# A decode attention kernel: the MLP spread over the first attention steps, K and V loaded in pairs

## The chip, the cores and the metric

One core of a Trainium2 chip. Times are device microseconds (us), medians of several executions. One profiled execution stands behind each trace; its span is about 2 us shorter than the time of the same execution (1378.4 us and 1380.39 us before).

## The reference

Two branches for 8 tokens, one per sequence, mixed by a gate. Branch A is attention over a cache: 32 heads, 4096 keys of 128, all bf16. The K cache and the V cache are 268 MB each. Branch B is a layernorm and an MLP (576 to 4608 to 576).

```python
q = (x @ wq).reshape(B, 1, 32, 128)                 # B = 8, x is [8, 1, 576]
scores = einsum("bhqd,bhkd->bhqk", q, k_cache) * 128 ** -0.5
a = einsum("bhqk,bhkd->bhqd", softmax(scores), v_cache) ... @ wo
b = gelu(layernorm(x) @ w1 + b1) @ w2 + b2          # w1 [576, 4608], w2 [4608, 576]
out = g * a + (1 - g) * b                           # g = sigmoid(sum(x * gate_w))
```

## The kernel before

An item is one (sequence, head): 1 MB of K and 1 MB of V, 256 items in all. K arrives with keys on the partitions, so TensorE transposes it (32 transposes an item) into PSUM, VectorE and ScalarE evacuate it (copy it to SBUF, the on-chip memory), and eight score matmuls follow. PV for an item (its softmax weights times V) runs LAG = 37 steps later, when the softmax of its sequence is done. `P.add` appends an operation to an engine's program together with the events it waits for; each engine runs its program strictly in order.

```python
NK = 5            # K slots of one item
NV = 6            # V slots of one item
...
# prologue, in program order; K loads go on the sync engine's queue, the rest on ScalarE's
dma wq -> w2reg ; dma w1 -> w1reg                    # ScalarE's queue
for n in range(min(NK, NITEM)):
    issue_k(n, waits=[])                             # sync engine's queue
...
# query projection (QT), 160 matmuls, waits for wq
P.add("act", lambda a: a.dma_start(w2_v, B_w2...), waits=[e_QT])     # w2 overwrites wq
# first MLP matmul (hT), 180 matmuls, waits for w1; GELU; second MLP matmul, waits for w2
...
for m in range(min(NV, NITEM)):                      # V slots lie where w1 and w2 were
    issue_v(m, waits=[ev_w2reg_free, ev_w1reg_free, e_mlp_sb])
...
def emit_T(n):                                       # transpose item n, then refill its slot
    ...
    if n + NK < NITEM:
        issue_k(n + NK, waits=[last_group_ev])
...
emit_T(0)
for s in range(last_step + 1):
    for (fn, b) in chain_at.get(s, []): fn(b)        # softmax of a sequence
    if s + 1 < NITEM: emit_T(s + 1)
    if s < NITEM: emit_S(s)                          # scores
    if 0 <= s - LAG < NITEM: emit_PV(s - LAG)        # frees a V slot: issue_v(m + NV)
# wo is loaded into the K slots after the last scores; final projection; output
```

(Cuts are marked; `dma wq -> ...` abbreviates the load calls.)

## Time and profile before

| what | value |
|---|---|
| time | 1380.15 us (1379.28 to 1381.33, 5 runs) |
| bytes moved by DMA | 559.55 MB |
| TensorE busy | 80% of the span |
| chain of waits that ended last | DMA 73%, TensorE 23% |

The page's view of 40 equal slices (34.5 us each) gives busy tenths for TensorE and the DMA engines, and the rate that the DMA engines moved:

```profile
PE   0789998888888888888888888888888888887335
...
DMA  9789999999999999999999999999999999999993
GB/s 332 268 335 425 418 389 425 425 424 425 425 426 425 425 426 424 426 425 425 425 425 425 424 426 424 424 422 419 420 423 422 420 418 425 418 421 357 420 420 167
```

The DMA row is full while TensorE has room, and the rate is flat at about 425 GB/s except at both ends. The chain of waits says the same: DMA has 73% of it, TensorE 23%. The view by stretches shows where the rate is lower. Each row gives the start and end of a stretch, its length, the busy time and count of each engine, and, in the last three columns, TensorE's granted clock, the DMA share and GB/s:

```profile
core 0: us, PE busy (x) PEld busy (x) DVE busy (x) ACT busy (x) POOL busy (x), PEclk, DMA share, GB/s
20.00:45.00 25.00, 10.31 (x160) 9.18 (x160) 1.27 (x1) 0.00 (x0) 0.00 (x0) 1.00 1.01 377
45.00:60.00 15.00, 11.43 (x180) 10.23 (x180) 0.00 (x0) 0.00 (x0) 0.00 (x0) 1.00 1.01 352
60.00:76.00 16.00, 12.63 (x107) 6.44 (x105) 4.88 (x11) 1.93 (x3) 0.00 (x0) 1.00 0.06 10
76.00:165.00 89.00, 80.10 (x1232) 60.50 (x1232) 54.07 (x83) 42.50 (x42) 0.00 (x0) 0.98 1.01 422
165.00:195.00 30.00, 27.89 (x492) 21.51 (x491) 18.38 (x31) 14.42 (x16) 0.00 (x0) 1.00 0.97 378
195.00:1200.00 1005.00, 855.83 (x14690) 690.29 (x14687) 380.23 (x581) 284.38 (x291) 0.00 (x0) 0.82 1.01 424
1200.00:1262.00 62.00, 52.22 (x944) 42.19 (x941) 22.79 (x34) 16.19 (x16) 0.00 (x0) 0.83 0.96 388
1262.00:1378.40 116.40, 49.74 (x1230) 39.94 (x1230) 4.25 (x11) 1.36 (x3) 0.00 (x0) 0.55 0.84 345
```

A way to read it: the kernel must move its bytes, and at 425 GB/s that takes 559.55 MB / 425 GB/s = 1316.6 us. The rest of the 1378.4 us, 61.8 us, is time in which the engines moved less than that. For one stretch the loss is length x (1 - rate / 425): 15.6 us at 60 to 76 us, 5.4 us at 1200 to 1262, about 22 us from 1262 to the end. This is a bookkeeping against the rate that the middle sustains, not a law: rates are rounded to 1 GB/s, which is 2.4 us over the long middle.

The 15.6 us are visible in order of time (columns: start, length, engine, line, operation, and in brackets the idle time before it with what ended it):

```profile
32.29 10.31 PE L366 MATMUL psum_all<-xT,w2reg 128*128 128x8 bf16 x160 [19.78 <-DMA w2reg<-in_A_wq_dram]
...
48.57 11.59 PE L383 MATMUL psum_all<-yT,w1reg 128*128 128x8 bf16 x180 [5.97 <-DMA w1reg<-in_B_w_dram]
...
62.02 0.44 ACT L399 ACTIVATE hb<-hb 128x288 f32<-128x288 f32 x1 [49.23 <-DVE hb L398]
...
63.10 0.59 PE L406 MATMUL psum_all<-w2reg,hT 128*8 128x512 bf16 x1 [2.94 <-DVE hT L401]
...
74.44 2.76 ACTq L305 DMA_DIRECT2D w2reg<-in_A_v_cache_dram  x5
```

The first MLP matmul starts when w1 lands (48.6 us), GELU comes at 62 us, the second matmul at 63.1 us, and only at 74.4 us does ScalarE issue the first V loads. All earlier loads were done by about 61 us: the five K slots were full and TensorE, still in the MLP, freed none. The queues were empty.

### The profile page before, as it was taken

To read this page: it belongs to the slowest core of one execution; us is meant where nothing else is said; L and a number is where in the kernel's file an instruction comes from. 1 tells how busy PE (TensorE), PEld (TensorE's weight loads), DVE (VectorE), ACT (ScalarE), POOL (GpSimd) and SP (SyncE) were. 2 spreads that over 40 slices of the span, in tenths; PEclk is the share of its full clock that TensorE was granted. 3 is DMA by queue.
4 is the path that set the end of the run, shared out by engine and by line. 5 is a ranking of instruction groups with operands and counts; after the bars stand their busy time and mean duration, and the time that the engine had idled before them with its cause. 6 is when DMAs were issued, how large, how long until landed. Compare 5 with 4: busy or idle time off the path is not lost.

```text
span 1378.4 us, 40050 instructions
## 1 busy us (share of the span) xinstructions
PE 1100.9 (80%) x19030; PEld 880.9 (64%) x19030; DVE 493.3 (36%) x762; ACT 364.1 (26%) x379; POOL 3.3 (0%) x12
## 2 busy tenths in 40 slices
PE   0789998888888888888888888888888888887335
PEld 0557777667667766767666666667666666766333
DVE  2146654343333433334333433334333343332000
ACT  0035543223222322223222232223222232222000
POOL 0000000000000000000000000000000000000000
PEclk9999998777887787778887788878888788877556
DMA  9789999999999999999999999999999999999993
GB/s 332 268 335 425 418 389 425 425 424 425 425 426 425 425 426 424 426 425 425 425 425 425 424 426 424 424 422 419 420 423 422 420 418 425 418 421 357 420 420 167
DMA packets 84002, 559.55 MB, mean 406 GB/s; under 512 B 8416, under 2 KB 17152, under 8 KB 17152
## 3 DMA queue, kind: packets, MB, share of 16 engines
q10 hardware_dynamic: 42752, 283.82, 49.8%
q1 hardware_dynamic: 40992, 273.18, 47.6%
q8 instruction: 149, 2.44, 0.6%
q0 software_dynamic: 96, 0.01, 0.0%
q14 instruction: 13, 0.11, 0.0%
HBM read 556.96 MB, written 0.01 MB: 404 GB/s over the span
## 4 chain that ended last, share of the span: by engine, by line
DMA 73%; PE 23%; ACT 2%; DVE 1%; issue 0%; ACTq 0%; DVEq 0%
DMA kregion<-in_A_k_cache_dram 63%; PE psum_all L487 16%; DMA w2reg<-in_A_v_cache_dram 7%; DMA w1reg<-in_B_w_dram 3%; PE psum_all L510 3%; PE psum_all L588 2%; ACT kregion L471 2%; PE psum_all L383 1%; PE psum_all L629 1%; PE psum_all L406 1%; ACT w1reg L545 0%; ACTq L305 0%; DVE kregion L472 0%; ACT w1reg L471 0%; PE psum_all L559 0%
## 5 line engine op out<-in xcount | busy, mean ns | idle before, releaser
L487 PE MATMUL psum_all<-identB,kregion 128*128 128x128 bf16 x8192 | 651.5, 249 | 169.9 <-DMA kregion<-in_A_k_cache_dram 147.0
L487 PEld LDWEIGHTS psum_all<-identB,kregion 128*128 128x128 bf16 x8192 | 583.3, 114 | 219.2 <-DMA kregion<-in_A_k_cache_dram 164.3
L472 DVE COPY kregion<-psum_all 128x1024 bf16<-128x1024 bf16 x687 | 459.5, 689 | 669.6 <-PE psum_all L487 662.3
L471 ACT COPY kregion<-psum_all 128x1024 bf16<-128x1024 bf16 x337 | 341.0, 1012 | 816.9 <-PE psum_all L487 803.2
L588 PEld LDWEIGHTS psum_all<-w1reg,w2reg 128*128 128x128 bf16 x6848 | 188.9, 98 | 152.9 <-issue 98.0
L588 PE MATMUL psum_all<-w1reg,w2reg 128*128 128x1 bf16 x6848 | 207.2, 164 | 52.0 <-DMA w2reg<-in_A_v_cache_dram 51.6
L510 PE MATMUL psum_all<-kregion,qmask 128*32 128x512 bf16 x2048 | 185.5, 439 | 0.0
L510 PEld LDWEIGHTS psum_all<-kregion,qmask 128*32 128x32 bf16 x2048 | 34.8, 98 | 34.0 <-issue 15.8
L588 PEld LDWEIGHTS psum_all<-w1reg 128*128 128x128 bf16 x1344 | 37.1, 98 | 29.4 <-issue 18.7
L588 PE MATMUL psum_all<-w1reg 128*128 128x1 bf16 x1344 | 40.7, 164 | 10.2 <-DMA w1reg<-in_A_v_cache_dram 10.2
L572 DVE RECIPROCAL rinv<-psum_all 128x32 f32<-128x32 f32 x8 | 2.9, 358 | 99.7 <-PE psum_all L569 99.7
L366 PE MATMUL psum_all<-xT,w2reg 128*128 128x8 bf16 (+1 forms) x160 | 10.3, 176 | 19.8 <-DMA w2reg<-in_A_wq_dram 19.8
L366 PEld LDWEIGHTS psum_all<-xT,w2reg 128*128 128x128 bf16 (+1 forms) x160 | 9.2, 107 | 20.9 <-DMA w2reg<-in_A_wq_dram 19.9
L383 PE MATMUL psum_all<-yT,w1reg 128*128 128x8 bf16 (+1 forms) x180 | 11.6, 176 | 6.0 <-DMA w1reg<-in_B_w_dram 6.0
L383 PEld LDWEIGHTS psum_all<-yT,w1reg 128*128 128x128 bf16 (+1 forms) x180 | 10.3, 107 | 7.3 <-DMA w1reg<-in_B_w_dram 6.1
L399 ACT ACTIVATE hb<-hb 128x288 f32<-128x288 f32 x1 | 0.4, 443 | 49.2 <-DVE hb L398 49.2
L406 PE MATMUL psum_all<-w2reg,hT 128*8 128x512 bf16 x36 | 10.4, 420 | 2.9 <-DVE hT L401 2.9
L374 DVE CAST qmask<-psum_all 128x256 bf16<-128x256 f32 x1 | 1.3, 1273 | 31.0 <-PE psum_all L366 31.0
L629 PE MATMUL psum_all<-kregion,oT_all 128*8 128x512 bf16 x32 | 10.9, 471 | 0.9 <-DVE oT_all L575 0.9
L471 ACT COPY w1reg<-psum_all 128x1024 bf16<-128x1024 bf16 x7 | 7.1, 1012 | 15.2 <-PE psum_all L559 15.2
L550 DVE TENSOR_SCALAR Rmat<-Emat,lpart 128x32 f32<-128x32 f32 x8 | 1.9, 241 | 25.0 <-ACT w1reg L545 25.0
L522 DVE TENSOR_REDUCE pmax<-psum_all 128x1 f32<-128x1024 f32 x8 | 9.7, 1218 | 2.6 <-PE psum_all L510 2.6
(72 smaller groups left out, 95.2 us busy)
## 6 DMA issues: line engine op xcount, KB each, us to landing
kregion<-in_A_k_cache_dram SPq DMA_DIRECT2D x256, 1024.0 KB, 21.9
w2reg<-in_A_v_cache_dram ACTq DMA_DIRECT2D x214, 1024.0 KB, 23.0
w1reg<-in_A_v_cache_dram ACTq DMA_DIRECT2D x42, 1024.0 KB, 23.4
w2reg<-in_B_w_dram ACTq DMA_DIRECT2D x1, 5184.0 KB, 19.0
w1reg<-in_B_w_dram ACTq DMA_DIRECT2D x1, 4608.0 KB, 42.1
kregion<-in_A_wo_dram SPq DMA_DIRECT2D x1, 4608.0 KB, 87.9
w2reg<-in_A_wq_dram ACTq DMA_DIRECT2D x1, 4096.0 KB, 28.2
w1reg<-in_B_w_dram ACTq DMA_DIRECT2D x1, 576.0 KB, 44.5
```

The lines of the kernel that those rows point to most:

```text
L366: e_QT = P.pe_write(lambda t, h=h, kc=kc, csz=csz: t.matmul(QT_ps[:, h * 8:h * 8 + B], lhsT=wq_v[0:csz, kc, h * Dh:(h + 1) * Dh], rhs=xT[0 ...
L383: e_hT = P.pe_write(lambda t, fc=fc, kc=kc, csz=csz: t.matmul(hT_ps[:, fc * 8:fc * 8 + B], lhsT=w1_v[0:csz, kc, fc * 128:(fc + 1) * 128], ...
L406: P.pe_write(lambda t, fc=fc: t.matmul(mlp_ps0[0:B, :], lhsT=hTv[:, fc, :], rhs=w2_v[:, fc, 0:512], start=(fc == 0), stop=(fc == NFC - 1)) ...
L471: return P.eng_read("act", lambda a, dst=dst, src=src: a.copy(dst, src), regions=[f"ring{r}"], waits=waits, pub=True)
L472: return P.eng_read("dve", lambda v, dst=dst, src=src: v.tensor_copy(dst, src), regions=[f"ring{r}"], waits=waits, pub=True)
L487: lambda t, r=r, jl=jl, j=j, kb=kb: t.transpose(ring[r][:, jl * 128:(jl + 1) * 128], kb[:, j, :], identB[:, :]),
L510: lambda t, q=q, i=i, jstart=jstart, b=b, h=h, sset=sset, kt=kt: t.matmul(S_ps[sset][32 * q:32 * q + 32, 512 * i:512 * i + 512], lhsT=qmas ...
L522: max_ev[b] = P.eng_read("dve", lambda v, b=b, sset=sset: v.tensor_reduce(pmax[:, b:b + 1], S_ps[sset][:, 0:1024], AX.X, ALU.max), regions ...
L550: R_ev[b] = P.add("dve", lambda v: v.tensor_scalar(Rmat[:, 32 * b:32 * b + 32], Emat[:, :], lpart[:, b:b + 1], None, ALU.mult), waits=[exp ...
L572: e1 = P.eng_read("dve", lambda v: v.reciprocal(rinv[:, 32 * b:32 * b + 32], acc[:, ACC_LBC:ACC_LBC + 32]), regions=["acc"], waits=[c4_ev[ ...
L588: lambda t, j=j, q=q, jj=jj, vb=vb, pt=pt, sl=sl, h=h: t.matmul(acc[:, 32 * sl + h:32 * sl + h + 1], lhsT=vb[:, j, :], rhs=pt[:, jj * 128 ...
L629: P.pe_write(lambda t, h=h: t.matmul(attn_ps0[0:B, :], lhsT=oT_v[:, h, 0:B], rhs=wo_v[:, h, 0:512], start=(h == 0), stop=(h == H - 1)), re ...
```

## The change

Intent: let TensorE begin with K at once and do the MLP in pieces between the first K items, so that the load queues always have work; and load K and V in pairs of heads, 2 MB each, into deeper buffers. wq moves into w1's region, w1 is loaded after the query projection, w2 gets its own region, and K pairs 2 and 3 wait for wq so that wq is not slowed.

```diff
-NK = 5
-NV = 6
+NKP = 4
+NVP = 4
+STEP_HT, STEP_GELU, STEP_MLP = 8, 16, 18
...
-    for n in range(min(NK, NITEM)):
-        issue_k(n, waits=[])
+    for kp in range(min(NKP, NPAIR)):
+        issue_k(kp, waits=([] if kp < 2 else [ev_wq]))
...
-        src = A_k_cache[bb, hh].rearrange("(p j) d -> p (j d)", p=128)
+        src = A_k_cache[bb, hh:hh + 2].rearrange("t (p j) d -> p t (j d)", p=128)
...
-        if n + NK < NITEM:
-            issue_k(n + NK, waits=[last_group_ev])
+        if n % 2 == 1 and (n // 2) + NKP < NPAIR:
+            issue_k((n // 2) + NKP, waits=[last_group_ev])
...                                     (V the same)
+    for n in range(min(NKT, NITEM)):
+        emit_T(n)                       # two items transposed before the query projection
+    prologue_QT()                       # then w1 and w2 are issued
...
+        for c in range(nchunk):         # 36 blocks of 128 hidden columns, 6 at a time
+            fcs = list(range(c * CH, min(NFC, (c + 1) * CH)))
+            pro_at.setdefault(STEP_HT + c, []).append(lambda fcs=fcs: prologue_hT(fcs))
+            pro_at.setdefault(STEP_MLP + c, []).append(lambda fcs=fcs: prologue_mlp(fcs))
+        pro_at.setdefault(STEP_GELU, []).append(prologue_gelu)
...
     for s in range(last_step + 1):
+        for fn in pro_at.get(s, []):
+            fn()
```

V pairs 0 and 1 (in w1's region) are issued after the last piece of the first matmul, pairs 2 and 3 (in w2's region) after the second.

## The prediction

> **What bounds the kernel now.** DMA bytes: the page counts 559.55 MB. By stretches (windows view): 0-60 us, 343 GB/s at a DMA share of 0.98; 60-76 us, 10 GB/s at 0.06; 76-182 us, 417 GB/s; 182-1240 us, 423 GB/s at 1.01; 1240-1262 us, 325 GB/s at 0.86; 1262-1357 us, 415 GB/s; 1357-1378 us, 32 GB/s. The chain of waits agrees: 73% DMA, 63% of it K loads. TensorE, 80% busy, works in the shadow of the loads: K and V of an item are 2.1 MB, 4.9 us at 425 GB/s, against 1085/256 = 4.2 us of matmul (transpose, score and PV groups). The Trainium skill (DMA: Bandwidth & Descriptors, Specifications) gives a fabric ceiling of 435 GB/s; the measured 423-425 is near it, so the middle has 2-3% to give at most.
>
> **What the change does.** (a) It moves the MLP (11.6 us first matmul, 3 us GELU, about 11 us second matmul) from the serial prologue into steps 8-23 of the K stage, and puts two K transposes before the query projection. (b) It joins K and V loads into pairs of 2 MB; a pair of slots is freed after its second item. Bytes and 8 KB rows stay. (c) Buffers grow from 5 K and 6 V items to 8 and 8. (d) w1 and w2 load after the query projection, K pairs 2 and 3 after wq.
>
> **What it is worth.** The gap at 60-76 us is the prize: there the five K slots are full, V waits for the MLP, and TensorE has not started on K. Afterwards K slots turn over from about 40 us while w1, w2 and K keep the queues filled: 15-16 us back. The rest of the MLP's 25 us was already covered by loads. Deeper buffers may recover 2-3 us of small losses (165-195 us, at 349-398 GB/s; 420 late).
>
> Against it: a bubble of about 2 us where wq lands and K pairs 2-3 are only then issued; 2-4 us in the K stage, where TensorE is already 4.8 of 5 us busy (2.6 us an item) and now also carries the MLP; 1 us at the end, where the last load brings two items. The end stays: 21 us after the last load, and the dip when K runs out.
>
> The pairs themselves I value at nothing: the engines show a share of 1.01 already, and where large wq pieces load beside K (16-28 us) the rate is about 427 GB/s, no better.
>
> Sum: 1380 - 15.5 - 2.5 + 4 = **1366 us**, range 1356 to 1374 (8 in 10). Chance of over 2% faster 0.12, within 2% 0.86, over 2% slower 0.02.
>
> **What would show it.** Right: no stretch near zero GB/s between 15 and 100 us; first PV at about 165-170 us instead of 184; the middle still at 423-425 GB/s; 20-22 us after the last load; mean DMA rate about 410 GB/s. If pairs mattered, the middle would run above 428. If the K stage became TensorE-bound, 100-180 us would fall below 400 GB/s.
>
> **What would make it wrong.** A middle 1% faster or slower with 2 MB loads is worth 11-13 us by itself. TensorE stalling in program order on w1 or w2 (steps 8 and 18) until the K slots are full would bring part of the gap back. The granted clock was 1.00 until about 215 us, then 0.82; if it drops earlier because TensorE works from 18 us on, the K stage loses several us.

## The result

The changed kernel takes 1365.82 us (1364.69 to 1366.2, 7 runs) against 1381.33 us for the kernel before in the same rounds (13 runs). The ratio is 0.9887, with a 95% interval of 0.9877 to 0.9898: 1.1% faster. A ratio here is the mean time of one kernel's runs over that of the other's of the same rounds, so it is not quite the ratio of the quoted medians.

The slices after (34.1 us each), and then the view by the same stretches (columns as before):

```profile
PE   3789998888878878888787988887888797887335
...
DMA  8999999999999999999999999999999999998993
GB/s 288 397 400 418 420 425 425 426 425 425 425 425 426 425 426 426 425 425 426 425 425 425 426 426 425 425 425 426 424 425 425 420 413 425 425 404 344 421 421 162
```

```profile
20.00:45.00 25.00, 13.33 (x188) 11.37 (x189) 2.08 (x3) 2.18 (x3) 0.00 (x0) 0.55 0.88 342
45.00:60.00 15.00, 14.58 (x223) 11.02 (x221) 9.79 (x15) 7.38 (x8) 0.00 (x0) 0.96 1.02 429
60.00:76.00 16.00, 6.55 (x95) 5.54 (x90) 2.67 (x4) 1.73 (x2) 0.00 (x0) 0.71 1.02 333
76.00:165.00 89.00, 83.95 (x1227) 62.51 (x1226) 47.97 (x77) 34.33 (x36) 0.00 (x0) 0.98 1.02 416
165.00:195.00 30.00, 28.19 (x539) 22.30 (x536) 16.55 (x27) 14.02 (x16) 0.00 (x0) 1.00 1.01 425
195.00:1200.00 1005.00, 831.84 (x14704) 679.58 (x14701) 379.69 (x583) 284.19 (x291) 0.00 (x0) 0.83 1.01 425
1200.00:1262.00 62.00, 49.98 (x959) 40.49 (x958) 20.39 (x33) 14.79 (x17) 0.00 (x0) 0.75 0.92 369
1262.00:1363.30 101.30, 38.91 (x1049) 31.96 (x1046) 2.27 (x5) 0.00 (x0) 0.00 (x0) 0.55 0.81 334
```

The second and third slices went from 268 and 335 to 397 and 400 GB/s; the chain of waits is still DMA's, 73%. The mean rate over the span rose from 406 to 410 GB/s. The losses by stretch, worked out as above from the two tables of stretches (the first 20 us lose 6.2 us in both):

| stretch, us | lost before, us | lost after, us | change |
|---|---|---|---|
| 20 to 45 | 2.8 | 4.9 | +2.1 |
| 45 to 60 | 2.6 | -0.1 | -2.7 |
| 60 to 76 | 15.6 | 3.5 | -12.2 |
| 76 to 165 | 0.6 | 1.9 | +1.3 |
| 165 to 195 | 3.3 | 0.0 | -3.3 |
| 195 to 1200 | 2.4 | 0.0 | -2.4, as large as the rounding |
| 1200 to 1262 | 5.4 | 8.2 | +2.8 |
| 1262 to the end | 21.9 | 21.7 | -0.2 |

The changes sum to -14.6 us; the spans differ by 15.1 us. The bytes are the same (559.52 MB), and the page's count of packets under 512 bytes fell from 8416 to 4320: 4096 fewer, 16 for each of the 256 loads that no longer exist.

Three rows of the timeline after explain the start: the query projection, the first piece of the MLP, and the first V loads:

```profile
30.30 10.31 PE L384 MATMUL psum_all<-xT,w1reg 128*128 128x8 bf16 x160 [10.66 <-DMA w1reg<-in_A_wq_dram]
...
72.19 1.98 PE L414 MATMUL psum_all<-yT,w1reg 128*128 128x8 bf16 x30 [9.45 <-DMA w1reg<-in_B_w_dram]
...
97.57 4.59 ACTq L319 DMA_DIRECT2D w1reg<-in_A_v_cache_dram  x2
```

The query projection starts at 30.3 us, when wq is in. TensorE then stands 9.4 us for w1 at 62 to 72 us, but in that stretch the DMA share is 1.02, so the stall costs nothing by itself. Issuing the first two V loads took ScalarE 4.59 us instead of 0.37 us each as in the middle. The first PV starts at 179.0 us, against 186.5 before.

### The profile page after: what moved, and what is told of

It is laid out like the page before. It is cut to its first block, busy times and chain, and to the rows that moved or that the text cites. A ratio compares the mean times of both kernels' runs of the same rounds, so it can differ in the third digit from the quotient of the medians.

```text
span 1363.3 us, 39656 instructions
## 1 busy us (share of the span) xinstructions
PE 1074.6 (79%) x19030; PEld 871.7 (64%) x19030; DVE 492.3 (36%) x762; ACT 364.3 (27%) x380; POOL 3.3 (0%) x12
## 2 busy tenths in 40 slices
DMA packets 79904, 559.52 MB, mean 410 GB/s; under 512 B 4320, under 2 KB 13056, under 8 KB 13056
## 4 chain that ended last, share of the span: by engine, by line
DMA 73%; PE 23%; ACT 2%; DVE 1%; ACTq 1%; issue 0%; DVEq 0%
DMA kregion<-in_A_k_cache_dram 62%; PE psum_all L530 14%; DMA w2reg<-in_A_v_cache_dram 7%; PE psum_all L631 3%; PE psum_all L553 3%; DMA w1reg<-in_B_w_dram 2%; DMA w1reg<-in_A_wq_dram 2%; ACT ktregion L510 1%; PE psum_all L414 1%; PE psum_all L384 1%; PE psum_all L693 1%; PE psum_all L444 1%; ACTq L319 0%; DVE ktregion L511 0%; PE psum_all L602 0%
## 5 line engine op out<-in xcount | busy, mean ns | idle before, releaser
L511 DVE COPY ktregion<-psum_all 128x1024 bf16<-128x1024 bf16 x687 | 458.8, 689 | 694.2 <-PE psum_all L530 687.2
L510 ACT COPY ktregion<-psum_all 128x1024 bf16<-128x1024 bf16 x337 | 341.0, 1012 | 828.9 <-PE psum_all L530 828.6
L553 PE MATMUL psum_all<-ktregion,qmask 128*32 128x512 bf16 x2048 | 178.2, 423 | 1.4 <-DVE qmask L392 1.4
L631 PEld LDWEIGHTS psum_all<-w1reg,w2reg 128*128 128x128 bf16 x4096 | 112.4, 98 | 89.1 <-issue 55.0
L631 PEld LDWEIGHTS psum_all<-w1reg 128*128 128x128 bf16 x4096 | 112.0, 98 | 86.0 <-issue 55.5
L631 PE MATMUL psum_all<-w1reg,w2reg 128*128 128x1 bf16 x4096 | 122.7, 164 | 33.7 <-DMA w2reg<-in_A_v_cache_dram 32.3
L631 PE MATMUL psum_all<-w1reg 128*128 128x1 bf16 x4096 | 122.2, 164 | 29.9 <-DMA w1reg<-in_A_v_cache_dram 29.9
L553 PEld LDWEIGHTS psum_all<-ktregion,qmask 128*32 128x32 bf16 x2048 | 34.4, 97 | 33.9 <-issue 12.6
L384 PE MATMUL psum_all<-xT,w1reg 128*128 128x8 bf16 (+1 forms) x160 | 10.3, 175 | 10.7 <-DMA w1reg<-in_A_wq_dram 10.7
L384 PEld LDWEIGHTS psum_all<-xT,w1reg 128*128 128x128 bf16 (+1 forms) x160 | 9.2, 107 | 11.9 <-DMA w1reg<-in_A_wq_dram 10.8
L510 ACT COPY w1reg<-psum_all 128x1024 bf16<-128x1024 bf16 x7 | 7.1, 1012 | 16.8 <-PE psum_all L602 16.8
## 6 DMA issues: line engine op xcount, KB each, us to landing
kregion<-in_A_wo_dram SPq DMA_DIRECT2D x1, 4608.0 KB, 92.2
```

What stands on the lines that cost most here:

```text
L384: e_QT = P.pe_write(lambda t, h=h, kc=kc, csz=csz: t.matmul(QT_ps[:, h * 8:h * 8 + B], lhsT=wq_v[0:csz, kc, h * Dh:(h + 1) * Dh], rhs=xT[0 ...
L510: return P.eng_read("act", lambda a, dst=dst, src=src: a.copy(dst, src), regions=[f"ring{r}"], waits=waits, pub=True)
L511: return P.eng_read("dve", lambda v, dst=dst, src=src: v.tensor_copy(dst, src), regions=[f"ring{r}"], waits=waits, pub=True)
L553: lambda t, q=q, i=i, jstart=jstart, b=b, h=h, sset=sset, kt=kt: t.matmul(S_ps[sset][32 * q:32 * q + 32, 512 * i:512 * i + 512], lhsT=qmas ...
L631: lambda t, j=j, q=q, jj=jj, vb=vb, pt=pt, sl=sl, h=h: t.matmul(acc[:, 32 * sl + h:32 * sl + h + 1], lhsT=vb[:, j, :], rhs=pt[:, jj * 128 ...
```

## The experiments

Twelve kernels ran. All gave the reference's result within the tolerance; one of them, rem128, computes part of it wrongly, which the comparison did not see. "Theory A" below is the prediction's: only empty load queues cost time. "Theory C" is its rival: the size of the loads or the depth of the buffers speeds up the middle.

### Parts of the change, one at a time

**split**: every 2 MB load becomes two of 1 MB, same moment, same slots, same release.

```diff
-        src = A_k_cache[bb, hh:hh + 2].rearrange("t (p j) d -> p t (j d)", p=128)
-        ... one dma_start of the pair
+        for t in range(2):
+            ... one dma_start of item 2 * kp + t, with its own semaphore      (V the same)
```

> The changed kernel with every 2 MB load issued as two loads of 1 MB, at the same moment, into the same slots, released in pairs as before. Theory A: nothing, 1364 to 1367 us, the middle at 422 to 425 GB/s. Theory C (the size of a load matters): 1372 us or more and a lower rate in the middle.

Measured: 1366.83 us, ratio to before 0.9897 (0.9884 to 0.9911); the middle (195 to 1200 us) at 425 GB/s, as after. The size of a load is worth nothing here. Theory C loses half of its ground.

**single**: no pairs at all; eight K and eight V slots of one item, each refilled as soon as it is free.

```diff
-        if n % 2 == 1 and (n // 2) + NKP < NPAIR:
-            issue_k((n // 2) + NKP, waits=[last_group_ev])
+        if n + 8 < NITEM:
+            issue_k(n + 8, waits=[last_group_ev])                             (V the same)
```

> The changed kernel with 1 MB loads, each issued as soon as its own slot is free (eight K and eight V slots, no pairs at all). Theory A: the loads of the middle stay the same, the dip where K runs out (1220 to 1250 us, 7.8 us lost with pairs, 5.4 us before) shrinks by 2 to 3 us: 1361 to 1364 us. Theory C: 1372 us or more.

Measured: 1365.13 us, ratio 0.9887 (0.9874 to 0.9901). It is no slower, so Theory C is out for pairs; but the expected 2 to 3 us at the end of K did not come: 1200 to 1262 us ran at 375 GB/s (7.3 us lost, against 8.2 with pairs and 5.4 before; the 7.8 us quoted above are for 1220 to 1250 us alone). The dip is not made by the pairs.

**shallow**: as single, but with the old depth of five K and six V slots. This is the spread MLP with the early transposes, and nothing else of the change.

```diff
+NKS = 5           # K slots of one item
+NVS = 6           # V slots of one item (slots 0 to 3 in w1's region, 4 and 5 in w2's)
```

> As the one before (1 MB loads, no pairs) but with the old depth, five K and six V slots: the spread MLP and the early transposes alone. Theory A: nearly the whole gain stays, 1365 to 1371 us; a little is lost to a longer bubble at 30 to 42 us and to the transition at about 175 us. Theory C (depth or size is the gain): 1375 us or more.

Measured: 1367.42 us, ratio 0.9902 (0.9887 to 0.9917), 13.8 us less than before in the same rounds by the medians, of about 15.5 for the whole change. The view by stretches of this run (columns as above):

```profile
20.00:45.00 25.00, 14.02 (x200) 12.03 (x200) 2.66 (x3) 1.71 (x3) 0.00 (x0) 0.52 0.82 304
45.00:60.00 15.00, 13.53 (x212) 9.75 (x209) 9.21 (x14) 7.87 (x8) 0.00 (x0) 1.00 1.02 395
60.00:76.00 16.00, 12.09 (x164) 9.85 (x164) 4.59 (x7) 3.01 (x3) 0.00 (x0) 0.79 1.02 395
165.00:195.00 30.00, 29.36 (x591) 23.18 (x588) 17.28 (x27) 12.14 (x12) 0.00 (x0) 1.00 0.99 401
1200.00:1262.00 62.00, 49.35 (x946) 39.61 (x944) 20.32 (x33) 14.52 (x16) 0.00 (x0) 0.78 0.95 386
```

The stretch at 60 to 76 us is filled (395 GB/s). A longer bubble appears at 20 to 45 us (304 GB/s, 7.1 us lost), because five slots hold too little to bridge the query projection. At 165 to 195 us 401 GB/s remain, and the end of K loses only 5.7 us. So depth gives back 2 to 3 us in one place and takes 2 to 3 in another. Spreading the MLP, with the early transposes, is nearly the whole gain; the two were not run apart at this depth. *single* and *shallow* differ in depth alone: 2.3 us by the medians, with intervals that overlap.

**serial**: the changed kernel, but with the MLP in one piece between the query projection and the K loop.

```diff
-STEP_HT, STEP_GELU, STEP_MLP = 8, 16, 18
+STEP_HT, STEP_GELU, STEP_MLP = 8, 16, 40      # takes the branch that runs the MLP at once
```

> The changed kernel with the MLP put back in one piece before the K loop (pairs, eight slots each and the two early transposes stay). Theory A, that only idle load queues cost time and anything that gives them work counts: ten K items (two early transposes free a pair) instead of five can be loaded while the MLP runs, about 5 MB or 12 us of the 15.6 us gap, but V still waits for it; a gap of 7 to 9 us is left at about 72 to 80 us: 1374 us, 1371 to 1377. Theory B, that spreading the MLP over the K steps is the whole gain: 1380 or more. Theory C, that 2 MB loads or deeper slots speed up the long middle: at most 1368.

Measured: 1374.96 us, ratio 0.9955 (0.9943 to 0.9968): less than half of the gain is left.

```profile
60.00:70.00 10.00, 5.11 (x80) 4.59 (x80) 0.00 (x0) 0.00 (x0) 0.00 (x0) 0.50 1.07 352
70.00:80.00 10.00, 7.06 (x104) 6.04 (x104) 2.45 (x6) 0.65 (x2) 0.00 (x0) 0.50 0.76 254
80.00:85.00 5.00, 5.00 (x30) 1.98 (x27) 0.00 (x0) 0.00 (x0) 0.00 (x0) 0.66 1.01 428
85.00:95.00 10.00, 10.00 (x123) 6.25 (x122) 3.73 (x7) 1.70 (x2) 0.00 (x0) 1.00 0.58 212
```

The queues run dry twice. At 76.5 us the first V pairs are issued, after the first matmul; at 91.3 us the other two, after the second. In between, nothing can be asked for. Theory A holds in its number; Theory B (no gain without the spread MLP) and Theory C (the full gain without it) do not.

**before_k7**: the kernel before with seven K slots instead of five.

```diff
-NK = 5
+NK = 7
```

> The kernel before with seven K slots instead of five, nothing else (more do not fit). Theory A: two more items, 2.1 MB, are loaded while the MLP runs: 4.9 us of the 15.6 us gap at 60 to 76 us is filled; the dip where K runs out grows by about 1 to 1.5 us with the deeper slots: 1376 to 1379 us, against about 1381 before. Rival (the gap is closed only by running K items during the MLP): 1380 to 1382 us.

Measured: 1378.31 us, ratio 0.9983 (0.9971 to 0.9996). The number is in the range, but the picture was not the expected one:

```profile
64.00:80.00 16.00, 13.06 (x114) 6.96 (x115) 3.58 (x9) 1.93 (x3) 0.00 (x0) 1.00 0.04 15
80.00:100.00 20.00, 16.57 (x240) 12.44 (x237) 10.86 (x17) 8.48 (x9) 0.00 (x0) 0.91 0.96 394
165.00:195.00 30.00, 27.67 (x477) 21.06 (x474) 19.41 (x31) 15.03 (x17) 0.00 (x0) 1.00 1.01 424
1200.00:1262.00 62.00, 49.97 (x925) 40.71 (x921) 21.11 (x32) 15.18 (x15) 0.00 (x0) 0.84 0.93 371
```

The empty stretch did not shrink; it moved from 60 to 76 us to about 64 to 80 us. The two extra K items travel beside wq and w1 and delay them: the first MLP matmul starts at 53.7 us instead of 48.6, the second at 68.2 instead of 63.1. The two items are in before the hole, but the hole ends as much later: 60 to 165 us lost 17.3 us, 16.2 before. The gain comes elsewhere, at 165 to 195 us (424 instead of 378 GB/s, 3.2 us), and the deeper end of K takes back 2.5 us (371 instead of 388 GB/s at 1200 to 1262 us); the rest lies in small differences and within the rounding of the middle. So the number was hit by luck. "Filling a gap" was the wrong picture for this one: a chain of dependent loads was stretched by what was loaded beside it.

### What the change left

**nowait**: K pairs 2 and 3 are issued at the start.

```diff
-        issue_k(kp, waits=([] if kp < 2 else [ev_wq]))
+        issue_k(kp, waits=[])
```

> The changed kernel with K pairs 2 and 3 issued at the start instead of after wq has landed. Theory A (the queues run dry at 25 to 35 us, 4.9 us lost there): most of it comes back, 1361 to 1364 us, and wq lands 1 to 3 us later without harm. Rival: the slow stretch there is the last piece of wq itself (64 rows onto 64 partitions), and only moves: 1365 to 1366 us.

Measured: 1368.42 us, ratio 0.991 (0.9896 to 0.9923), about 3 us slower than the changed kernel (by the ratios of different rounds). A miss. Views of this run by stretches, the start of the query projection, and ScalarE in the issue of the first V loads:

```profile
30.00:45.00 15.00, 8.77 (x139) 7.88 (x139) 0.00 (x0) 0.00 (x0) 0.00 (x0) 0.50 0.98 348
45.00:50.00 5.00, 3.63 (x44) 2.56 (x43) 1.31 (x2) 1.49 (x2) 0.00 (x0) 0.50 0.50 144
```

```profile
36.23 10.31 PE L384 MATMUL psum_all<-xT,w1reg 128*128 128x8 bf16 x160 [17.60 <-DMA w1reg<-in_A_wq_dram]
...
93.40 9.22 ACTq L319 DMA_DIRECT2D w1reg<-in_A_v_cache_dram  x2
102.66 1.01 ACT L510 COPY ktregion<-psum_all 128x1024 bf16<-128x1024 bf16 x1 [10.58 <-issue]
```

The query projection starts at 36.2 us instead of 30.3, because wq now shares the engines with more K. By 45 us everything that could be asked for is loaded (wq and five K pairs), and w1 is issued only after the query projection, at 46.6 us: the queue is dry at 45 to 50 us (144 GB/s). The bubble only moved: 20 to 76 us lose 8.2 us in all, 8.3 in the changed kernel, and the chain from wq to w1 became 6 us longer. The 3 us are lost later. From 76 to 165 us 4.0 us are lost instead of 1.9: the issue of the first V loads, behind w2 in the same queue, held ScalarE for 9.2 us instead of 4.6, TensorE stood 7.3 us for the copy after it, V pairs 2 and 3 were issued at 140.2 us instead of 137.5, and 135 to 140 us ran at 182 GB/s instead of 349. From 1200 us to the end 31.9 us are lost instead of 29.9; why stays open. So the wait acts as a priority for wq, and removing it cost time; that the order of the loads costs the 3 us by itself is not shown.

**early_wo** and **early_sp**: theory D says that the dip at the end of K comes from the deep K buffer. When the last K load is issued, eight items are still to be computed; these steps are bound by TensorE, and only V asks for loads, one item a step. So wo was issued earlier, from ScalarE's queue, then from the sync engine's.

```diff
+            if s + 1 == NITEM - 8 + 4:             # after the transposes of item 252
+                P.add("act", dma wo, waits=[T_last_ev[252]])        # early_sp: "sp"
...
-    P.add("sp", dma wo, waits=[T_last_ev[255], S_done_ev[255]] + ...)
```

> The changed kernel with the load of wo issued as soon as the transposes have left the slots that it overwrites (after item 252), from the V queue, instead of after the last score matmul from the K queue. Theory D, formed after the run without pairs did not shorten the dip at 1220 to 1250 us: with eight K slots full the last eight steps are bound by TensorE and only V asks for loads, one item a step, so the depth makes the dip and not the pairs. Then work for the queues shortens it: about 3 to 4 us of the 7.8 us come back, 1361 to 1363 us, and wo lands near 1270 us instead of 1339. If the dip were a limit of the loads themselves: 1365 to 1366 us.

> As the early wo before, but issued from the K queue (the sync engine). In the run before, ScalarE stood 9.8 us in the issue of a V load behind wo, and TensorE waited 11 us for its evacuation. Theory E: that stall ate the gain; from an engine with nothing else to do, the dip at 1220 to 1250 us gets wo as filling: 1361 to 1364 us, the fast end if all of it works. Rival (an early wo takes from V what it gives): 1365 to 1366 us.

Measured: 1365.47 us, ratio 0.9886 (0.9872 to 0.9899), and 1366.27 us, ratio 0.989 (0.9873 to 0.9907). Neither gained. From ScalarE's queue wo landed 27.5 us after its issue instead of 92.2, but this is in the timeline of early_wo:

```profile
1237.34 16.79 ACTq L319 DMA_DIRECT2D w2reg<-in_A_v_cache_dram  x1
...
1254.17 1.01 ACT L510 COPY ktregion<-psum_all 128x1024 bf16<-128x1024 bf16 x1 [17.77 <-issue]
...
1255.24 3.06 PE L530 MATMUL psum_all<-identB,kregion 128*128 128x128 bf16 x27 [10.94 <-ACT ktregion L510]
```

The issue of the next V load, behind wo in the same queue, held ScalarE for 16.8 us (the copy after it had waited 17.8 us on nothing else), and TensorE stood 10.9 us for that copy. From the sync engine no engine stalled, but wo took 94.5 us. The counts of packets (`--dma` with a window) show why the load with 1152-byte rows is slow beside one with 8 KB rows: from 1265 to 1300 us of the changed kernel wo's queue moved 1660 packets and V's 1661, but 1.91 MB and 12.77 MB (before, 1265 to 1320 us: 2731 and 2729). Packet for packet, wo gets 1152 / (1152 + 8192) of 425 GB/s, an estimate of 52 GB/s or 90 us for its 4.7 MB. It is not a fixed share: early_sp had 1052 against 2029 at 1260 to 1300 us. The stretch 1235 to 1260 us was better filled (402 to 427 GB/s after 1240 us), yet the same bytes came out short later, at 1310 to 1340 us (wo landed at 1329 us, beside the last V loads). So the dip can be filled and no time is won: Theory D's picture of the dip agrees with the depths tried (5.4 and 5.7 us lost with five slots, 7.3 to 9.2 with seven or eight), but what an early wo would be worth without these side effects stays open.

**best** and **best2**: take the final projection out of the end. The last sequence is normalised and projected in groups of heads while V still loads. best also has nowait and wo from ScalarE's queue; best2 has the K wait of the changed kernel, and wo from the sync engine.

```diff
+    GROUPS = [(0, 8), (8, 16), (16, 24), (24, 28), (28, 30), (30, 32)]
...
+                if m_ == (B - 1) * H + h1_ - 1: emit_norm(g_)     # m_: the PV just emitted
+                if m_ == (B - 1) * H + h1_ and h1_ < H: emit_proj(g_)
```

> All together: K pairs 2 and 3 at the start, the early wo, and the final projection taken out of the end: the last batch is normalised and projected in groups of heads while V still loads, so that only two heads are left after the last load. From theory A the 21 us between the last load and the end are on the path in full, as no load is left to hide them: some 8 us remain, 12 to 13 us gained there; with 3 us each from the other two: 1344 to 1350 us. If the end were hidden or set by something else, 1358 or more.

> The changed kernel (its K pairs 2 and 3 still wait for wq) with the wo load from the sync engine after item 252, and the last batch normalised and projected in groups of heads while V loads. The run before of this kind ended 8 us after its last load was seen instead of 17, so 1351 to 1356 us: 9 to 10 us less than the changed kernel from the end, 0 to 4 from wo.

Measured: best 1359.47 us, ratio 0.9844 (0.983 to 0.9857); best2 1364.66 us, ratio 0.9876 (0.986 to 0.9892). Both missed their numbers. The mechanism is there: from the last wait for V to the end it took 17 us before (1361.4 to 1378.4) and after (1346.6 to 1363.3), and 8 us in best (1349.4 to 1357.3). That is 9 us, where the expectation counted 12 to 13, because it took the end from the fall of the rate and not from the last wait. And best was run together with nowait and early_wo, before it was known that the first costs 3 us and the second gains nothing, where the expectation counted 3 us gained from each. In best2 the first group had to wait for wo. One row of its list of waits (total us, times, longest):

```profile
PE psum_all L646 <- DMA kregion<-in_A_wo_dram: 19.5, 1, 19.5
```

While TensorE stood for wo, it freed no V slots, and the queue ran dry (34 GB/s at 1305 to 1310 us).

**rem128**: the last 64 rows of w1 are loaded as 128 half rows onto all 128 partitions; the matmuls read the wrong half.

```diff
-e.dma_start(w1_v[0:REM, KC_FULL, :], B_w1[KC_FULL * 128:D, :])
+e.dma_start(w1_v[:, KC_FULL, 0:F // 2], B_w1[KC_FULL * 128:D, :].rearrange("r (t x) -> (r t) x", t=2))
```

> Wrong result on purpose: in the changed kernel the last 64 rows of w1 (0.59 MB) are loaded as 128 half rows onto all 128 partitions instead of 64 rows onto 64 partitions; same bytes. If the slow stretch at 60 to 70 us (352 and 233 GB/s at full DMA share) comes from writing to half of the partitions, it goes: about 420 GB/s until w2 starts, and 1.5 to 3 us less, 1363 to 1364.5 us. If it comes from something else in that stretch (the small rows of w2), it stays and the time too.

Measured: 1363.24 us (1361.91 to 1365.24), ratio 0.9864 (0.9845 to 0.9883). By the medians that is 2.6 us less than the changed kernel, though the two intervals just overlap, and the profiled execution, the slowest of the four, has the changed kernel's span (1363.4 and 1363.3 us): what the slow stretch no longer loses there is lost in small amounts in other stretches. So the gain in time is likely, not shown. The end of the slow stretch itself is clear, first in the changed kernel, then in this one:

```profile
65.00:69.00 4.00, 0.00 (x0) 0.00 (x0) 0.00 (x0) 0.00 (x0) 0.00 (x0) 0.71 1.01 222
```

```profile
65.00:69.00 4.00, 0.00 (x0) 0.00 (x0) 0.13 (x1) 0.00 (x0) 0.00 (x0) 1.00 1.01 416
```

At a DMA share of about 1 in both, the rate at 65 to 69 us nearly doubled. The Trainium skill (SBUF — State Buffer, "Door 1: The DMA port swizzle") says that partitions 0 to 63 reach only 8 of the 16 ports, with an asymptote of about 218 GB/s. This case agrees in direction: with the load spread over all partitions the stretch runs at nearly the full rate. The 222 GB/s do not test the 218: they are the sum of all that moved, 0.59 MB from K's queue and 0.30 MB from w1's and w2's in 4 us (`--dma` with this window), and K, in the other queue, was slowed as well (1.23 MB in rem128). The half rows are also half as long (4608 bytes); that this plays no part was not tested.

**best4**: the three things that survived, together: the groups (20, 6, 4 and 2 heads); wo from ScalarE's queue but only after ScalarE's last work for others; and the 64-row pieces of wq and w1 on all partitions, with the transposed inputs spread over even and odd partitions so that the result is right.

```diff
+    GROUPS = [(0, 20), (20, 26), (26, 30), (30, 32)]
+        if s == NITEM + 6:
+            P.add("act", dma wo, waits=[T_last_ev[NITEM - 1]])
+    # rows 512.. of w1 (and of wq) as in rem128; the last 64 columns of y (and x) are
+    # transposed into partitions 2r (left half of the columns) and 2r + 1 (right half), zeros elsewhere
+    lhsT=w1_v[:, KC_FULL, (fc % 18) * 128:(fc % 18 + 1) * 128], rhs=yTr[:, fc // 18, 0:B]
```

> The changed kernel with three things that the runs before suggest. One: wo is issued from the V queue, but only after the last work that ScalarE has for other engines, so that a stalled issue holds up nobody, and lands near 1300 us. Two: the last batch is normalised and projected in groups of 20, 6, 4 and 2 heads while V loads (8 us after the last load instead of 17). Three: the last 64 rows of wq and w1 are loaded as 128 half rows onto all partitions, this time with the matmuls changed so that the result is right. Expected: 8 to 9 us from the end, 2.6 us from w1 as in the run with the wrong result, 1 to 2 us from wq: 1352 to 1356 us. If the end again gives only 5 us: 1357 or more.

Measured: 1354.58 us (1354.41 to 1354.69), ratio to before 0.9813 (0.98 to 0.9827). It is correct and beats both kernels: 26 us less than before, 10 to 11 us less than the changed kernel (other rounds). wo landed 29.9 us after its issue, and the last wait for V ended 9.0 us before the end. The three were not run apart in this form; by stretches the end (from 1262 us) lost 13.7 us against 21.7 in the changed kernel, 20 to 45 us 2.6 against 4.9, and 60 to 76 us 0.2 against 3.5, but 76 to 165 us 4.2 against 1.9. It is not the last word. In its timeline of ScalarE stands

```profile
83.50 13.38 ACTq L323 DMA_DIRECT2D w1reg<-in_A_v_cache_dram  x2
96.92 1.01 ACT L522 COPY ktregion<-psum_all 128x1024 bf16<-128x1024 bf16 x1 [13.81 <-issue]
```

two V loads whose issue, behind w2's small rows, held ScalarE for 13.4 us and TensorE with it.

## Why the prediction was right

The time was predicted at 1366 us and came out at 1365.82. Point by point:

- **DMA bytes bound the kernel, and the empty stretch was the prize.** Right, and shown: the whole stretch from 45 to 76 us lost 18.2 us before and 3.3 after, 14.9 us, against 15 to 16 predicted. *shallow* shows that the spread MLP with the early transposes alone brings almost all of it, *serial* that without the spread less than half remains.
- **Pairs are worth nothing.** Right, and shown by *split* and *single*. The Trainium skill (DMA: Bandwidth & Descriptors, "Measured" under Bandwidth) gives 341 GB/s for a load of 1 MB and 425 for one of 16 MB, issued from GpSimd; here loads of 1 MB from ScalarE and SyncE, with several queued (*split*, *single*), ran at 425 in the middle. The measured case decides: with a full queue the size of the single load does not show.
- **A bubble of about 2 us near wq.** Right in size (2.1 us more lost at 20 to 45 us). That removing the wait would win it back, as thought after the result, was wrong (*nowait*).
- **K stage, 2 to 4 us.** Somewhat less: 1.3 us at 76 to 165 us. The stall on w1 that the prediction named as a risk came, 9.4 us of TensorE, and cost no load time, because the DMA engines were busy with just that load.
- **Deeper buffers, 2 to 3 us.** 3.3 us at 165 to 195 us, of which about half is not depth (*shallow*, with the old depth, lost 1.7 there), and perhaps 2.4 in the middle, which is within the rounding: the two kernels with five K slots showed 424 and 423 GB/s there, those with more slots 424 or 425.
- **The end, 1 us more.** The end itself stayed (17.0 and 16.7 us after the last wait for V). The dip before it grew by 2.8 us. The prediction put it down as unchanged; it goes with the depth.
- **First PV at about 165 to 170 us.** Wrong: 179.0 us. The largest piece that the timeline shows is the wait for w1, 9.4 us. ScalarE's 4.6 us in the issue of V held TensorE for little (1.2 us at most in one wait), and *early_wo*, where the same two issues took 0.9 us, has its first PV at 177.3 us. The clock's part is small: the 32 transposes after the query projection took 3.49 us, the next 2.03. The Trainium skill (TensorE: Matmul & The Clock Gate, Part 1) has the array fall to half clock after an idle window of about 3.4 us; this trace agrees, the clock going from 1.00 at 15 to 20 us to 0.50 at 25 to 30 us while TensorE waited for wq. This is not the drop that the prediction feared, which was to come from work. And it is no loss against before, though the column says 1.00 there. The query projection took 10.31 us in both kernels (rows at 32.29 and 30.30 us above). In the trace before, the matmuls of 512 columns at 63 to 66 us took 0.61 us and the same ones after 66.2 us 0.38, while the column stayed at 1.00: at the start of a trace, check it against the durations. All of this moved the time little (76 to 165 us lost 1.9 us), since the loads went on.

So the sum was right with two terms too small and opposite in sign (depth in the middle, depth at the end), and with TensorE's part of the story wrong where it mattered little. By the table, 45 to 76 us gave 14.9 us (15.5 predicted), 165 to 1200 us 5.7 (2.5 predicted, 2.4 of it within the rounding), and the rest cost 6.0 (4 predicted). The mechanism was right; that the two misses cancel, so that the time came within 0.2 us, is luck.

## What to carry to other kernels

When loads bound a kernel, count the bytes at the sustained rate and list the stretches that fall short: each is a moment when nobody could ask for more, and the question there is which engine's program order, slot or dependent load kept the next request back. Here work moved off such a stretch paid nearly its full length, and larger loads paid nothing, as the queue was full. Before removing a wait or reordering loads, ask which load the next requests hang on, and before issuing a load from a compute engine, ask what that engine owes to others if the issue itself stalls.

## What the Trainium skill lacked or had wrong

- DMA: Bandwidth & Descriptors gives no time for which an issue can hold the issuing engine; under "Issuing engines are not separate DMA queues" it calls the time to initiate a DMA usually small relative to the DMA itself. Here the issue of a 2 MB load by ScalarE took 0.37 us in the middle; for the first two V loads behind w2 it took 0.9 us (early_wo, issued at 98.1 us), 4.6 (the changed kernel, 97.6 us), 9.2 (nowait, 93.4 us) and 13.4 (best4, 83.5 us), and 16.8 us for one behind wo (w2 and wo have rows of 1152 bytes). TensorE stood 10.9 us for it in early_wo.
- The same page's "Arbitration" says that each engine takes turns between queues by packets. What it means for a load with small rows beside one with large rows is not said: wo (1152-byte rows) took 92.2 us from issue to landing beside V (8 KB rows) in the other queue (1660 packets against 1661 at 1265 to 1300 us), and 27.5 us in V's own queue.
- The same page's rule "Batch DMAs to ≥1 MiB for ≥75% of peak" and its 341 GB/s for 1 MB (issued from GpSimd) do not carry over to loads in a full queue: with loads of 1 MB queued the runs show 425 GB/s, and 2 MB loads no more. Its "HBM-per-NC limit" of about 358 GB/s was passed through the middle, at 425 GB/s on one core; under "Measured" the page itself gives that figure for both cores of a pair streaming.
- SBUF — State Buffer gives the rates of loads on part of the partitions; what such a load does to one on all 128 partitions beside it is not said. Here all queues together fell to 222 GB/s while 64 rows went to 64 partitions (K's queue moved 0.59 MB in 4 us), and ran at 416 (K 1.23 MB) when they went to 128.
